# The 512-key tiles of P: transposed in the rounded type after a transfer from SBUF to SBUF

## The chip, the cores and the metric

The kernel runs on one core of a Trainium2 chip. The metric is the device time of one execution, in microseconds (us). Before the change it is 824.83 us, the median of 3 runs that lie between 823.99 and 824.9 us.

Five instruction streams run side by side: PE (TensorE, matmuls and their weight loads), DVE (VectorE), ACT (ScalarE), POOL (GpSimd) and SP (SyncE, which here only issues DMA transfers). Each works its own list strictly in the order in which it was written, and waits on semaphores for the others.

## The reference

Block-causal attention (blocks of 64 positions), then a feed-forward block whose gate comes from a convolution over three positions. All of it is float32, and the shapes are 8 batches, 8 heads, 576 positions, 64 features per head, and 1024 hidden features.

```python
scores = 1/sqrt(64) * q @ k.T                 # per batch and head: 576 x 576
scores = where(block_i >= block_j, scores, -1e9)
attn = softmax(scores) @ v                    # max taken off first, exp, divided by the row's sum
x = concat of the heads                       # 576 x 512 per batch
h = maximum(x @ w_in, 0)                      # 576 x 1024
conv = sum over k of conv_w[k] * h shifted by k - 1
out = (h * sigmoid(conv)) @ w_out             # 576 x 512
```

## The kernel before, in words

**Precision.** TensorE multiplies in the rounded type (float32r in the code, `F32R`), so most operands are held as a rounded part "h" and a remainder "l", and a product is the sum of two or three matmuls over these parts.

**Attention.** The work goes by pairs of heads. A head's queries are cut into blocks of 128: block i (0 to 3) sees 128(i+1) keys, so block 3 sees 512 keys; the last 64 queries of both heads of a pair form a fifth block of 576 keys. For a block, two matmuls make the scores in a PSUM bank (lines 709 and 711), DVE writes the mask (714) and takes the row maximum (717), ACT takes the exponential and its row sum (720) into an SBUF tile `p0` to `p4` in plain float32, DVE sums and inverts (671, 676), and POOL multiplies the tile by the inverse in place (682). These tiles are called P here. Then `one_bank` (from line 786) transposes P: TensorE takes each chunk of 128 keys as the stationary operand and an identity (`ident`, float32) as the moving one, with `is_transpose` set (791), into a PSUM bank; ACT evicts the bank as the rounded part (801) and DVE subtracts to get the remainder (804). The matmuls with the values read these (868). A tile of 512 keys is transposed in 4 chunks; there are 64 such tiles, one for each head and batch, in all 256 transposes out of some 800 at line 791.

**Stages.** The first batch is treated in two parts, queries 0 to 255 of all four pairs ("A") and then the rest ("B"), while the weights arrive and are decoded. The other 28 pairs are done whole. The 512-key tiles of the first batch belong to part B. The feed-forward matmuls of a batch (lines 936 and 993) are spread between the attention work of the next batch; those of the last batch end the program.

**What sets the order.** Each operation is entered in a plan with its engine, an estimated duration and latency, its dependences and a due time; `Plan.order` (line 94) then sorts all of it into one list per engine. The constants from line 224 on (`SLOT`, `OX`, `WOFF` and so on) set the due times. A tile taken from `one` has a single buffer, one from `two` has two, and the next user of a buffer depends on every user of the tile before it. Where the plan sees TensorE idle for longer than `LEAST` = 0.45 us, it puts in transposes of the identity that nobody reads (line 1110, called fillers here); there are 274 of them.

**DMA.** Nearly all transfers are issued from SP: the loads of q, k and v, the moves of rounded parts between partitions of SBUF (599, 608, 621) and the stores of the output (1006). A transfer that waits for its source holds up all that stand behind it on SP.

Of the kernel before, what the change touches and what calls it, by code (L numbers as in the profile page):

```python
# [193 lines left out]
def kernel(  # L194
# [26 lines left out]

    Q1 = 256

    SLOT, SLOTA, SLOTB = 10.87, 3.37, 5.12
    WOFF, WSTEP, WLEAD = 8.21, 4.0, 6.0
    WOFF2, WSTEP2 = 38.72, 3.23
    OXA, OPVA, OTA = 1.86, 3.32, 0.58
    OXB, OPVB, OTB = 5.65, 14.0, 3.99
    OX, OPV, OT = 8.41, 18.92, 6.21
    VLEAD, NLEAD, NB, CONV = 4.98, 4.48, 2.78, -20.45  # L230
    OFA, OFB, OF, OXS = 2.97, 9.83, 2.14, 1.25
    FA, FB = 51.86, 92.46
    TAIL1 = ('f', 's')
    TAIL2 = ('pt', 'tv')
    EBLK = (2,3)
    SKIP = 5.0
    LEAST, SPARE = 0.45, 0.2
    GROUPS = {"A": ((0, 1),), "B": ((2,), (3,)), None: ((0, 1, 2), (3,))}
    NORMS = {"A": (0,1), "B": (2,4), None: ()}
    VACT = True  # L240
    XDIRECT = True
    WDVE = ()
    WINDOW = 33.68

    cp = ctx.enter_context(tc.tile_pool(name="cp", bufs=1))
    p2 = ctx.enter_context(tc.tile_pool(name="p2", bufs=2))
# [43 lines left out]
    def c_pool(n, two_in=False):  # L290
        return 0.1 + n * 0.0022 if two_in else 0.16 + n / 1200.0

    ident = cp.tile([P, P], F32, tag="ident", name="ident")
    make_identity(nc, ident)
    nident = cp.tile([P, P], F32R, tag="nident", name="nident")
    nc.scalar.activation(out=nident, in_=ident, func=AF.Copy, scale=-1.0)
    wih = cp.tile([P, NCC, DFF], F32R, tag="wih", name="wih")
# [358 lines left out]
    def stage_s(ops, hh, at, part, shared):  # L656
# [9 lines left out]
        def finish(blocks, st, c0, t0):  # L666
            a, b_, w_ = c0 + blocks[0], c0 + blocks[-1] + 1, 2 if blocks[0] < 4 else 3

            def i1():
                x = 4 if blocks[0] == 4 else 4 + 2 * blocks[0]  # L670
                nc.vector.tensor_reduce(out=st.ap[:, a:b_],
                                        in_=st.ap[:, x:x + w_ * (b_ - a)].rearrange("p (n w) -> p n w", w=w_),
                                        op=ALU.add, axis=AX.X)

            def i2():
                nc.vector.reciprocal(st.ap[:, a:b_], st.ap[:, a:b_])  # L676

            o = pl.op(DVE, 0.15, i1, t0, deps=exps[4] if blocks[0] == 4 else [exps[x] for x in blocks], bufs=[st])
            o = pl.op(DVE, 0.12, i2, t0, deps=[o], bufs=[st])
            for x in blocks:  # L680
                def norm(pt=pb[x], col=c0 + x):
                    nc.gpsimd.tensor_scalar(out=pt.ap, in0=pt.ap, scalar1=st.ap[:, col:col + 1], scalar2=0.0,  # L682
                                            op0=ALU.mult, op1=ALU.add)

                w = 128 * (x + 1) if x < 4 else S
                if x in NORMS[part]:
                    def norm_a(pt=pb[x], col=c0 + x):
                        nc.scalar.activation(out=pt.ap, in_=pt.ap, func=AF.Copy, scale=st.ap[:, col:col + 1])  # L688

                    done[x] = pl.op(ACT, c_act(w, False, True), norm_a, t0 + 0.3, deps=[o], bufs=[st, pb[x]])  # L690
                    continue
                done[x] = pl.op(POOL, c_pool(w) + 0.08, norm, t0 + 0.3, deps=[o], bufs=[st, pb[x]])

        groups = GROUPS[part]
        for z, i in enumerate(i for g in groups for i in g):
            nk = 128 * (i + 1)
            pt = two([P, nk], F32, f"p{i}")
            pb[i] = pt
            t0 = at + (0.6 if part == "A" else 1.3) * z
            sb = bank("f" if part == "A" and i else "s")  # L700
# [74 lines left out]
    def stage_x(pbd, hh, at, part, shared):  # L775
# [10 lines left out]
        def one_bank(trs, rows, n, hi, lo, deps, t0, bufs_p, bufs_hi, bufs_lo, sub_ok, tag, shape):  # L786
            tb = bank(tag)

            def tr():
                for z, (x, c, kk, col) in enumerate(trs):  # L790
                    nc.tensor.matmul(tb.ap[0:kk, col:col + P], pb[x].ap[:, 128 * c:128 * c + kk], ident,  # L791
                                     start=(z == 0), stop=True, is_transpose=True, skip_group_check=True)

            o = pl.op(PE, len(trs) * 0.109, tr, t0, deps=deps, bufs=[tb] + bufs_p)

            def src():
                x = tb.ap[0:rows, 0:n]
# [348 lines left out]
```

## Time and profile before

| | |
|---|---|
| median of the runs | 824.83 us |
| the profiled execution's own time | 826.01 us |
| its span, first to last instruction | 824.2 us |
| PE busy / its weight loads busy | 805.8 us / 736.6 us |
| DVE / ACT / POOL busy | 658.5 / 634.0 / 437.9 us |
| granted TensorE clock, mean over the span | 0.995 |
| DMA: moved, mean rate | 96.09 MB, 117 GB/s |
| SP's DMA queue: share of the 16 engines | 47.3% |

A row of the profile names the line of the code, the engine, the operation, what is written and read (`w<-ident,p` is the transpose of P into a bank `w`), the shapes and the count, then busy time, the mean of one instruction in ns, and idle time ahead of it. Matmuls overlap each other, so the mean length of one (some 270 ns for a transpose) isn't what it costs; the distance from start to start is. That distance is read from the timeline, where equal neighbours are merged: n matmuls that together last T, each of length L, started (T - L)/(n - 1) apart.

### The profile page before, as it was taken

The page shows a single profiled execution, that of the slowest core. Times are in us where ns is not written, and L with a number is a line of the kernel's source. Part 1 is how long each engine was busy: PE and PEld are TensorE (multiplying, and loading weights), DVE is VectorE, ACT ScalarE, POOL GpSimd, SP SyncE. Part 2 cuts the span into 40 slices and gives each one's busy share as a digit, 9 for nine tenths or more (in the row PEclk, how much of TensorE's full clock was granted, in tenths as well). Part 3 has the DMA queues.
Part 4 walks back from the last instruction along what each step waited for, and adds up shares of the span by engine and source line. Part 5 has one row for each costly group of instructions (what it writes and reads, how often), then busy time and mean ns, then how long its engine had stood idle before and what let it go on. Part 6 is the DMA issues. An engine that isn't in the chain of part 4 may idle for free.

```text
span 824.2 us, 17518 instructions
## 1 busy us (share of the span) xinstructions
PE 805.8 (98%) x5531; PEld 736.6 (89%) x5531; DVE 658.5 (80%) x1945; ACT 634.0 (77%) x1800; POOL 437.9 (53%) x579
## 2 busy tenths in 40 slices
PE   7999899999999999999999999999999999999997
PEld 6888778988999989999999989999999989999996
DVE  5899887998997967889797967889797977887541
ACT  5789887887896967878796967878796967877651
POOL 2456566564565645546555645546565645645421
PEclk9999999999999999999999999999999999999999
DMA  9364756556555544444556444445556434430001
GB/s 234 113 155 104 183 159 157 131 126 147 146 119 145 117 103 107 106 113 114 145 119 146 108 113 103 106 114 117 145 119 144 116 91 113 93 99 14 14 26 40
DMA packets 168096, 96.09 MB, mean 117 GB/s; under 512 B 136748, under 2 KB 142404, under 8 KB 168004
## 3 DMA queue, kind: packets, MB, share of 16 engines
q1 hardware_dynamic: 165924, 94.44, 47.3%
q8 instruction: 45, 0.74, 0.4%
q10 hardware_dynamic: 2080, 0.52, 0.4%
q14 instruction: 47, 0.39, 0.2%
HBM read 38.82 MB, written 9.44 MB: 59 GB/s over the span
## 4 chain that ended last, share of the span: by engine, by line
PE 90%; DVE 3%; SPq 2%; ACT 2%; DMA 2%; issue 1%; POOL 0%; ACTq 0%; DVEq 0%
PE f L936 24%; PE f L993 21%; PE w L868 12%; PE w L791 10%; PE s L709 5%; PE s L711 5%; PE w L582 4%; PE w L993 3%; PE s L747 3%; PE s L936 2%; PE s L1110 1%; DMA xh<-in_moe_w_out_dram 1%; SPq L372 1%; DMA kn<-in_k_dram 1%; DMA ka<-kh 1%
## 5 line engine op out<-in xcount | busy, mean ns | idle before, releaser
L682 POOL TENSOR_SCALAR p<-p,st 128x512 f32<-128x512 f32 (+4 forms) x260 | 144.3, 570 | 158.6 <-DVE st L676 73.1
L974 POOL TENSOR_TENSOR gl<-t,gh 128x288 fp32r<-128x288 f32 (+2 forms) x128 | 103.9, 816 | 127.4 <-ACT gh L971 101.2
L720 ACT ACTIVATE p<-s,st 128x128 f32<-128x128 f32 (+1 forms) x248 | 131.2, 529 | 36.2 <-DVE st L717 31.0
L791 PE MATMUL w<-ident,p 128*128 128x128 f32 (+1 forms) x800 | 126.6, 275 | 1.9 <-DVE kl L589 1.4
L717 DVE TENSOR_REDUCE st<-s 128x1 f32<-128x128 f32 (+1 forms) x248 | 120.4, 486 | 4.0
L801 ACT ACTIVATE ptbh<-w 128x512 fp32r<-128x512 f32 (+2 forms) x192 | 94.5, 509 | 26.5 <-PE w L791 25.5
L791 PEld LDWEIGHTS w<-ident,p 128*128 128x128 f32 (+1 forms) x800 | 95.3, 140 | 12.9 <-ACT p L688 1.9
L993 PE MATMUL f<-woh,gh 128*128 128x512 f32 x248 | 105.8, 427 | 0.0
L936 PE MATMUL f<-xh,wih 128*128 128x290 f32 (+2 forms) x480 | 101.7, 312 | 0.4 <-ACT stage L1003 0.3
L804 DVE TENSOR_TENSOR ptbl<-w,ptbh 128x512 fp32r<-128x512 f32 (+1 forms) x144 | 89.9, 633 | 14.8 <-ACT ptbh L801 14.3
L936 PE MATMUL f<-xh,wil 128*128 128x290 f32 (+2 forms) x480 | 99.2, 310 | 0.0
L993 PE MATMUL f<-woh,gl 128*128 128x512 f32 x248 | 98.2, 396 | 0.0
L993 PE MATMUL f<-wol,gh 128*128 128x512 f32 x248 | 98.1, 395 | 0.0
L936 PE MATMUL f<-xl,wih 128*128 128x290 f32 (+2 forms) x480 | 96.0, 305 | 0.0
L711 PE MATMUL s<-kl,qz 128*128 128x128 f32 (+1 forms) x240 | 78.0, 325 | 0.0
L936 PEld LDWEIGHTS f<-xh,wih 128*128 128x128 f32 x480 | 74.1, 189 | 3.9 <-DVE t L967 0.6
L955 DVE SCALAR_TENSOR_TENSOR t<-f,cw,t 128x287 f32<-128x287 f32 (+3 forms) x120 | 59.0, 492 | 20.6 <-ACT t L951 19.4
L936 PEld LDWEIGHTS f<-xl,wih 128*128 128x128 f32 x480 | 73.8, 190 | 0.8
L936 PEld LDWEIGHTS f<-xh,wil 128*128 128x128 f32 x480 | 73.2, 190 | 0.3
L889 DVE TENSOR_TENSOR xt<-w,xt 64x256 f32<-64x256 f32 x112 | 51.3, 460 | 27.2 <-ACT xt L886 24.6
L886 ACT ACTIVATE xt<-w 64x256 f32<-64x256 f32 x112 | 44.8, 402 | 23.0 <-PE w L868 18.4
L868 PE MATMUL w<-ptbh,vv 128*128 128x320 f32 (+3 forms) x288 | 62.3, 320 | 0.0
(161 smaller groups left out, 2054.7 us busy)
## 6 DMA issues: line engine op xcount, KB each, us to landing
kn<-in_k_dram SPq DMA_DIRECT2D x64, 144.0 KB, 2.9
ka<-kh SPq DMA_DIRECT2D x64, 144.0 KB, 2.7
kb<-kh SPq DMA_DIRECT2D x64, 144.0 KB, 2.6
out_dram<-stage SPq DMA_DIRECT2D x36, 256.0 KB, 2.3
vn<-in_v_dram SPq DMA_DIRECT2D x64, 128.0 KB, 2.6
qn<-in_q_dram SPq DMA_DIRECT2D x56, 144.0 KB, 2.7
qa<-qh SPq DMA_DIRECT2D x28, 144.0 KB, 3.1
qa<-ql SPq DMA_DIRECT2D x28, 144.0 KB, 3.1
```

Of the source, the lines that this page charges most:

```text
L682: nc.gpsimd.tensor_scalar(out=pt.ap, in0=pt.ap, scalar1=st.ap[:, col:col + 1], scalar2=0.0, op0=ALU.mult, op1=ALU.add)
L711: nc.tensor.matmul(sb.ap[:, 0:nk], qz.ap[:, z:z + 128], kl.ap[:, 0:nk], start=False, stop=True)
L717: nc.vector.tensor_reduce(out=st.ap[:, i:i + 1], in_=sb.ap[:, 0:nk], op=ALU.max, axis=AX.X, negate=True)
L720: nc.scalar.activation(out=pt.ap[:, 0:nk], in_=sb.ap[:, 0:nk], func=AF.Exp, bias=st.ap[:, i:i + 1], accum_out=st.ap[:, 4 + 2 * i:5 + 2 * i])
L791: nc.tensor.matmul(tb.ap[0:kk, col:col + P], pb[x].ap[:, 128 * c:128 * c + kk], ident, start=(z == 0), stop=True, is_transpose=True, skip_ ...
L801: nc.scalar.activation(out=hi(), in_=src(), func=AF.Copy)
L804: nc.vector.tensor_tensor(out=lo(), in0=src(), in1=hi(), op=ALU.subtract)
L868: nc.tensor.matmul(tb.ap[0:m, q0 - qa:qb - qa], vv.ap[:, chunk(c), hh, w[ps_]], pm.ap[:, 128 * c + q0:128 * c + qb] if qa == 0 else pm.ap[ ...
L936: nc.tensor.matmul(fb.ap[:, 0:n2], wt[:, c, fs], xs[c][xi].ap[:, x0:x0 + n2], start=(n + c - c0 == 0), stop=(n + c - c0 == 3 * NCC - 1))
L955: nc.vector.scalar_tensor_tensor(out=t.ap[:, i0:no], in0=fb.ap[:, own + i0 - 1:own + no - 1], scalar=cw[:, f:f + 1], in1=t.ap[:, i0:no], o ...
L974: nc.gpsimd.tensor_tensor(out=gbuf[1].ap[:, f, carry:carry + no], in0=t.ap[:, 0:no], in1=gbuf[0].ap[:, f, carry:carry + no], op=ALU.subtract)
L993: nc.tensor.matmul(fb.ap[:, 0:DM], gbuf[a].ap[:, f, cs], w[:, f, :], start=(f == 0 and n == 0), stop=(f == NFC - 1 and n == 2))
```

## The change

P's tiles in `RAW`, which are those of 512 keys, get one step more. After POOL has normalized the tile, SP issues a transfer of all of it (128 partitions of 2 KB) from SBUF to SBUF, into a tile `pr3` that is declared in the rounded type; the bytes are the same. The transposes of that tile read `pr3` and a second identity, `rident`, in the rounded type, and write their PSUM bank through a view in that type. The tile `p3` now has one buffer in place of two, and `pr3` has one. What reads the bank afterwards is as it was.

The plan books 0.65 us on SP for the transfer and 2.6 us more until it has landed, and 0.087 us in place of 0.109 us for one of these transposes. The due times were set anew as well, and so the lists of all engines differ in many places.

```diff
-    SLOT, SLOTA, SLOTB = 10.87, 3.37, 5.12
+    SLOT, SLOTA, SLOTB = 10.69, 3.13, 5.12
...
+    RAW = (3,)
...
+    rident = cp.tile([P, P], F32R, tag="rident", name="rident")
+    nc.scalar.activation(out=rident, in_=ident, func=AF.Copy)
...
                 done[x] = pl.op(POOL, c_pool(w) + 0.08, norm, t0 + 0.3, deps=[o], bufs=[st, pb[x]])
+                if x in RAW:
+                    pr = one([P, w], F32R, f"pr{x}")
+
+                    def over(pt=pb[x], pr=pr):
+                        nc.sync.dma_start(out=pr.ap.bitcast(F32), in_=pt.ap)
+
+                    done[x] = pl.op(SP, 0.65, over, t0 + 1.0, deps=[done[x]], bufs=[pb[x], pr], lat=2.6)
+                    pb[x] = pr
...
-            pt = two([P, nk], F32, f"p{i}")
+            pt = (one if i in RAW else two)([P, nk], F32, f"p{i}")
...
-                    nc.tensor.matmul(tb.ap[0:kk, col:col + P], pb[x].ap[:, 128 * c:128 * c + kk], ident,
-                                     start=(z == 0), stop=True, is_transpose=True, skip_group_check=True)
-
-            o = pl.op(PE, len(trs) * 0.109, tr, t0, deps=deps, bufs=[tb] + bufs_p)
+                    to = tb.ap[0:kk, col:col + P]
+                    raw = x in RAW and pb[x].args[2] == F32R
+                    nc.tensor.matmul(to.bitcast(F32R) if raw else to, pb[x].ap[:, 128 * c:128 * c + kk],
+                                     rident if raw else ident, start=(z == 0), stop=True, is_transpose=True, skip_group_check=True)
+
+            o = pl.op(PE, len(trs) * (0.109 if trs[0][0] not in RAW else 0.087), tr, t0, deps=deps, bufs=[tb] + bufs_p)
```

The counts by kind are the same on both sides but for these: 256 transposes change their operands, SP has 64 transfers more, ACT has one copy more (`rident`), and the fillers go from 274 to 257. Three places show what moved. They lie around one tile, that of the first head in the third pair of the fifth batch; line numbers of the changed kernel are 4 to 14 higher.

PE, the rows up to the transposes of that tile, before (`s` banks take scores, `w_6986` and `w_6992` are banks for transposes, `p3_6898` is the tile):

```order
L709 MATMUL s_6963<-kb_6710,qb_6639 128x128
L711 MATMUL s_6963<-kl_6594,qz0_96 128x128
L993 MATMUL f_6969<-woh_85,gh_1138 128x512
L993 MATMUL f_6969<-wol_86,gh_1138 128x512
L993 MATMUL f_6969<-woh_85,gl_1189 128x512
L582 MATMUL w_6979<-ident_76,kn_6734 128x96 x3
L791 MATMUL w_6986<-ident_76,p0_6852 128x128
L791 MATMUL w_6986<-ident_76,p1_6866 128x128 x2
L791 MATMUL w_6992<-ident_76,p3_6898 128x128 x4
L709 MATMUL s_7003<-kb_6710,qb_6639 128x256
```

And in the changed kernel:

```order
L805 MATMUL w_7019<-ident_76,p0_6902 128x128
L805 MATMUL w_7019<-ident_76,p1_6916 128x128 x2
L721 MATMUL s_7029<-kb_6758,qb_6689 128x128
L723 MATMUL s_7029<-kl_6662,qz0_98 128x128
L1007 MATMUL f_7034<-woh_87,gh_1159 128x512
L1007 MATMUL f_7034<-wol_88,gh_1159 128x512
L1007 MATMUL f_7034<-woh_87,gl_1182 128x512
L586 MATMUL w_7045<-ident_76,kn_6814 128x96 x3
L721 MATMUL s_7053<-kb_6758,qb_6689 128x256
L723 MATMUL s_7053<-kl_6662,qz0_98 128x256
L805 MATMUL w_7060<-rident_81,pr3_6993 128x128 x4
```

The transposes of `p0` and `p1` moved ahead, and one pair of score matmuls of 256 keys now stands before the tile's transposes rather than behind them. Between the tile's own scores and these rows the two lists hold the same matmuls otherwise.

POOL at the same tile, before and then in the changed kernel (`gl` is the remainder of the gated activations, `st` the inverses):

```order
L974 TENSOR_TENSOR gl_1189<-t_6839,gh_1138 128x288
L682 TENSOR_SCALAR p0_6852<-p0_6852,st0_92 128x128
L682 TENSOR_SCALAR p1_6866<-p1_6866,st0_92 128x256
L682 TENSOR_SCALAR p2_6878<-p2_6878,st0_92 128x384
L682 TENSOR_SCALAR p3_6898<-p3_6898,st0_92 128x512
```

```order
L686 TENSOR_SCALAR p0_6902<-p0_6902,st0_94 128x128
L686 TENSOR_SCALAR p1_6916<-p1_6916,st0_94 128x256
L686 TENSOR_SCALAR p2_6930<-p2_6930,st0_94 128x384
L988 TENSOR_TENSOR gl_1182<-t_6893,gh_1159 128x288
L686 TENSOR_SCALAR p3_6954<-p3_6954,st0_94 128x512
```

A subtraction for the feed-forward block now stands between the normalization of `p2` and that of `p3`.

SP, from the loads of the values to the moves for the next pair of heads, before and in the changed kernel:

```order
L335 DMA vn_6792<-in_v_dram 64x2x64 x2
L319 DMA qn_6942<-in_q_dram 96x6x64 x2
L621 DMA qa_6961<-qh_6890 64x576
L621 DMA qa_6961<-ql_6900 64x576
L621 DMA qb_6983<-ql_6900 64x576
```

```order
L339 DMA vn_6838<-in_v_dram 64x2x64 x2
L701 DMA pr3_6883<-p3_6820 128x512
L701 DMA pr3_6993<-p3_6954 128x512
L625 DMA qa_7005<-qh_6977 64x576
L625 DMA qa_7005<-ql_6989 64x576
```

The transfers of two tiles, that of the head before and this one, stand between the loads of the values and the moves for the next pair, and the load of the following pair's q, which stood there, comes behind those moves.

More of the change, by code (lines that the diff above doesn't have):

```diff
@@ L222 @@
     Q1 = 256
-    SLOT, SLOTA, SLOTB = 10.87, 3.37, 5.12
[L225 to L232, printed above, removed]
+    SLOT, SLOTA, SLOTB = 10.69, 3.13, 5.12
+    WOFF, WSTEP, WLEAD = 6.38, 4.22, 5.72
+    WOFF2, WSTEP2 = 39.52, 3.2
+    OXA, OPVA, OTA = 3.87, 3.53, 0.33
+    OXB, OPVB, OTB = 4.55, 14.0, 3.99
+    OX, OPV, OT = 8.48, 18.92, 6.36
+    VLEAD, NLEAD, NB, CONV = 3.96, 7.21, 3.37, -20.45
+    OFA, OFB, OF, OXS = 2.97, 9.83, 2.14, 2.05
+    FA, FB = 61.7, 86.99
     TAIL1 = ('f', 's')
     TAIL2 = ('pt', 'tv')
+    RAW = (3,)
     EBLK = (2,3)
-    SKIP = 5.0
+    SKIP = 5.16
     LEAST, SPARE = 0.45, 0.2
@@ L242 @@
     WDVE = ()
-    WINDOW = 33.68
+    WINDOW = 36.23
     cp = ctx.enter_context(tc.tile_pool(name="cp", bufs=1))
```

## The prediction

> **What bounds the kernel now.** I read the page first, then the windows, to see in which stage TensorE is the bound.
>
> ```profile
> PE 805.8 (98%) x5531; PEld 736.6 (89%) x5531; DVE 658.5 (80%) x1945; ACT 634.0 (77%) x1800; POOL 437.9 (53%) x579
> PE   7999899999999999999999999999999999999997
> PE 90%; DVE 3%; SPq 2%; ACT 2%; DMA 2%; issue 1%; POOL 0%; ACTq 0%; DVEq 0%
> ```
>
> PE is busy in 98% of the span, and the chain of work that ended last runs over PE for 90%. "Busy" can hide waiting, so I split the span at 140 us, where the last long run of fillers has ended; the second answer is of the fillers (line 1110) alone, the third of PE's groups between 140 and 750 us.
>
> ```profile
> 0.00:140.00 140.00, 126.28 (x926) 111.26 (x927) 115.60 (x354) 110.60 (x301) 73.72 (x79) 0.98 0.64 157
> 140.00:750.00 610.00, 609.69 (x4213) 563.72 (x4212) 513.57 (x1528) 487.24 (x1413) 340.04 (x472) 1.00 0.50 118
> ```
>
> ```profile
> 0.00:140.00 140.00, 37.45 (x271) 32.62 (x271) 0.98 0.64 157
> 140.00:750.00 610.00, 0.52 (x3) 0.32 (x3) 1.00 0.50 118
> ```
>
> ```profile
> L791 PE MATMUL w<-ident,p 128*128 128x128 f32 (+1 forms) x683 | 106.4, 273 | 0.1
> ```
>
> The columns are the window, PE, its weight loads, DVE, ACT and POOL, each busy time and count, then clock and DMA. Up to 140 us PE idles for 14 us and runs 271 fillers: chains through the other engines set the pace there. From 140 to 750 us it is busy for 609.69 of 610 us with 3 fillers, its transposes waited 0.1 us in all, and the clock is full. What is left after 750 us is matmuls of the last batch. So a nanosecond taken off PE between 140 and 750 us comes off the end, as long as no new wait eats it; one taken off before 140 us mostly doesn't.
>
> **What one transpose costs now.** From the timeline, a group of four transposes with its weight loads and what follows:
>
> ```profile
> 404.32 0.49 PEld L791 LDWEIGHTS w<-ident,p 128*128 128x128 f32 x4
> 404.45 0.60 PE L791 MATMUL w<-ident,p 128*128 128x128 f32 x4
> 404.81 0.51 PE L936 MATMUL f<-xh,wil 128*128 128x290 f32 x2
> 409.69 0.41 PE L582 MATMUL w<-ident,qn 96*128 96x96 f32 x3
> ```
>
> ```profile
> L582 PE MATMUL w<-ident,qn 96*128 96x96 f32 x168 | 23.0, 245 | 0.4 <-issue 0.4
> ```
>
> One lasts 0.273 us, so four started (0.60 - 0.273)/3 = 0.109 us apart. The transposes of q (line 582, 0.245 us each) have as many weight columns, 128, but 96 moving ones: (0.41 - 0.245)/2 = 0.082 us. Per moving column that is 0.85 ns in both; so in float32 the moving side is the limit, and a float32 weight load of 128 columns needs no more than 0.082 us.
>
> **What one costs in the rounded type: the disputed term.** The trace of before has no such transpose. Three rows or pairs of rows bound it:
>
> ```profile
> 403.96 0.22 PE L709 MATMUL s<-ka,qa 128*128 128x128 f32 x1
> 404.02 0.27 PE L711 MATMUL s<-kl,qz 128*128 128x128 f32 x1
> 404.13 0.48 PE L936 MATMUL f<-xh,wil 128*128 128x290 f32 x2
> ...
> 70.79 0.53 PEld L808 LDWEIGHTS w<-ptbh,nident 128*128 128x128 f32 x4
> 70.91 0.56 PE L808 MATMUL w<-ptbh,nident 128*128 128x128 f32 x4
> ```
>
> ```profile
> L808 PEld LDWEIGHTS w<-ptbh,nident 128*128 128x128 f32 x56 | 7.8, 190 | 2.0 <-ACT ptbh L801 1.6
> ```
>
> The page writes f32 for both types here; lines 709, 711 and 808 multiply in the rounded one. A rounded matmul with 128 moving columns needs 0.06 us when its weights are in place (403.96 to 404.02). With weights of its own, the next starts 0.11 us on (to 404.13), and line 808's loads follow each other by (0.53 - 0.190)/3 = 0.113 us: the rounded weight load is the limit there, at 0.11 us. So 0.06 us is the floor, if in transpose mode the rounded load is as quick as the float32 one, and 0.111 us the ceiling, if it is as slow as at line 808. Both rows are equally near (the floor shares the mode of the load, the ceiling its type), and I take the middle, 0.086 us: 0.023 us saved, between 0.049 saved and 0.002 lost. A page of the Trainium skill, TensorE: Matmul & The Clock Gate, speaks against any gain in its section on LDWEIGHTS: a load takes the columns divided by 1.2 ns, 107 ns for 128. Line 808 agrees with it at 0.113 us and line 582 doesn't, with at most 0.082 us; held to strictly, it gives the second rival's time.
>
> **The change part by part.**
>
> Transposes. The tiles of 512 keys that POOL normalizes between 140 and 750 us, and the others of that line, stand in one row:
>
> ```profile
> L682 POOL TENSOR_SCALAR p<-p,st 128x512 f32<-128x512 f32 x54 | 37.8, 701 | 5.0 <-DVE st L676 4.9
> ```
>
> 54 tiles with 4 transposes are 216; 216 x 0.023 = **5.0 us** off the path (bounds: 10.6 off, 0.4 on). The other 40 run before 140 us and count nothing; their 0.9 us lie under the chains of that stage.
>
> Fillers. The lists have 17 fewer: 17 x 0.109 = **1.9 us** less idle time that is filled. This holds only if the idle time itself went, so I keep 0 to 3 us for it.
>
> The transfer's time. It moves 256 KB in 128 rows. Nearest rows, with the median from issue to landing:
>
> ```profile
> ka<-kh SPq DMA_DIRECT2D x64, 144.0 KB, 2.7
> out_dram<-stage SPq DMA_DIRECT2D x36, 256.0 KB, 2.3
> qa<-qh SPq DMA_DIRECT2D x28, 144.0 KB, 3.1
> ```
>
> ```profile
> 402.10 0.58 SPq L1006 DMA_DIRECT2D out_dram<-stage  x1
> 405.28 0.54 SPq L1006 DMA_DIRECT2D out_dram<-stage  x1
> 414.31 0.89 SPq L319 DMA_DIRECT2D qn<-in_q_dram  x2
> ```
>
> The same shape to DRAM takes 2.3 us, moves within SBUF 2.7 to 3.1. I take 2.7 us, 0.55 of which is the issue on SP. SP has room: between 405.82 and 414.31 us it issues nothing.
>
> Whether that is hidden. What hides it is the PE work between a tile's scores and its transposes. The chain of the tile shown in the part on the change, before:
>
> ```profile
> 431.91 0.39 PE L711 MATMUL s<-kl,qz 128*128 128x512 f32 x1
> 432.53 0.69 DVE L717 TENSOR_REDUCE st<-s 128x1 f32<-128x512 f32 x1
> 433.26 0.69 ACT L720 ACTIVATE p<-s,st 128x512 f32<-128x512 f32 x1
> 434.08 2.07 POOL L682 TENSOR_SCALAR p<-p,st 128x128 f32<-128x128 f32 x4 [0.16 <-PE w L868]
> 438.60 0.93 PE L791 MATMUL w<-ident,p 128*128 128x128 f32 x7
> 439.29 0.37 PE L709 MATMUL s<-kb,qb 128*128 128x256 f32 x1
> 439.61 0.39 PE L993 MATMUL f<-woh,gh 128*128 128x512 f32 x1
> ```
>
> The four normalizations end at 436.15, 4.24 us after the scores start; the tile's transposes are the last four of the seven, at 438.60 + 3 x 0.109 = 438.93, 7.0 us after. So 2.8 us were spare, and nothing waited. In the changed list one pair of 256-key scores is added ahead (439.29 to 439.61, 0.32 us): 7.3 us. But POOL now has a subtraction ahead of the tile's normalization, whose price has this row:
>
> ```profile
> L974 POOL TENSOR_TENSOR gl<-t,gh 128x288 fp32r<-128x288 f32 x92 | 74.4, 812 | 91.1 <-ACT gh L971 71.5 <-issue 19.1
> ```
>
> 4.24 + 0.81 + 2.7 = 7.75 us, against 7.3: PE would wait about 0.4 us. This is the tightest place; its pattern comes twice (fifth and seventh batch), which puts **0.8 us** back. Counted in the same way on the lists, with each matmul at its distance from the timeline, the other heads of the stage have 7.7 to 10.8 us between scores and transposes, mostly about 9. A usual chain, that of another head:
>
> ```profile
> 407.98 0.39 PE L711 MATMUL s<-kl,qz 128*128 128x512 f32 x1
> ...
> 411.76 0.70 POOL L682 TENSOR_SCALAR p<-p,st 128x512 f32<-128x512 f32 x1
> ```
>
> It has its norm at 412.46, 4.5 us after the scores, and with the transfer needs 7.2 us: 1.8 us spare. If that cover were gone, each of the 54 tiles would show its 2.7 us on PE.
>
> What stands behind the transfer on SP are the moves of q for the next pair, and the scores at line 709 wait for these:
>
> ```profile
> 437.09 0.51 SPq L621 DMA_DIRECT2D qa<-qh  x1
> ```
>
> ```profile
> 448.98 0.22 PE L709 MATMUL s<-ka,qa 128*128 128x128 f32 x1
> ```
>
> In the old run they went out at 437.09, after the norm's end at 436.15 us, and were needed 11.9 us later, so a transfer ahead of them costs nothing. SP's 64 issues of some 0.55 us, 35 us, lie in such gaps as the one above. The copy for `rident` falls into the start, where the loads are waited for: nothing, and on the path less than the 0.69 us of the 512-column row of ACT.
>
> Sum against the profiled execution (826.01 us, 1.2 us above the median): -5.0 - 1.9 + 0.8 = -6.1 us, 819.9 us. Against the median of 824.83 us: **818.7 us**.
>
> **The rivals.**
>
> 1. *The rounded load is quick in transpose mode*: 0.06 us each. 216 x 0.049 = 10.6 us; 824.8 - 10.6 - 1.9 + 0.8 = 813.1 us. For it: line 582's loads, in that mode, keep within 0.082 us. Against: no rounded load anywhere in the trace is below 0.11.
> 2. *No gain on PE*: the load stays at 0.111 us as at line 808, or the rounded type is moved at float32's rate, 0.109. 824.8 + 0.4 - 1.9 + 0.8 = 824.1 us.
> 3. *The transfer is the new wait, slower*: PE works its list in order, so a tile that lands late stops all of PE at the 54 places. The price is 54 times the mean shortage; with 6.1 us to lose, it turns the sign at 0.11 us of mean shortage. It would come where SP is just issuing a pair of loads ahead of the transfer (0.89 us for two at 414.31), the transfer lands in 3.1 us and a subtraction of 0.81 us has slipped in on POOL: 0.9 + 0.4 + 0.8 = 2.1 us, 0.3 more than the usual spare. A mean shortage of 0.3 us gives 824.8 - 6.9 + 16.2 = 834.1 us. Against: SP's idle stretch, and the distance from scores to transposes, whose median on the lists goes from 6.8 to 9.0 us.
>
> 4. *The single buffer of `p3` stops the early stage.* There the scores of two heads come close:
>
> ```profile
> 58.94 0.40 PE L711 MATMUL s<-kl,qz 128*128 128x512 f32 x1
> ...
> 63.45 0.40 PE L711 MATMUL s<-kl,qz 128*128 128x512 f32 x1
> ```
>
> 4.5 us apart, and an exponential starts 1.35 us after its scores (431.91 to 433.26), so the second one would find `p3` taken until 7.2 us after the first scores: it waits 7.2 - 4.5 - 1.35 = 1.35 us, and ACT with it, on 8 heads up to 11 us: 824.8 - 6.9 + 11 = 828.9 us. Against: the fillers of that stage show idle time that can take it. Its chance is in that of rival 3.
>
> **How the numbers follow.** The forecast has 45% (its own range 815 to 822 us), the quick load 20%, no gain 20%, the two late cases 15%. The range from 811 to 826.5 us takes in the first three and little of the last. A measurement of this kernel can tell 0.2%, 1.65 us, from no change, so faster means below 823.2 us: nearly all of the first two and, since 824.1 us lies so near the border, 7 points of the third, 72%. Within 0.2%: 12%. Slower: 16%.
>
> **What would show it.** Starts of the new transposes: 0.086 us apart if the forecast is right, 0.06 or 0.11 if a rival is. PE between 140 us and the last batch: still no wait on `pr3`, but for two tiles with some 0.4 us; rows "PE w <- DMA pr3" with over 6 us in all would mean rival 3. The transfer: 2.3 to 3.1 us to landing. The first 140 us: a 512-key score in the first whole pair not later than now. The forecast falls if the starts are at 0.11 or if the steady stage shows waits for the transfer.

## The result

The changed kernel takes 834.85 us (median of 4 runs, 832.25 to 837.3) beside 824.87 us of the kernel before on the same chip (823.99 to 825.07): 1.0123 times the time, 95% interval 1.0087 to 1.0158. It is slower by 10 us, 1.2%. The prediction was 818.7 us, and its range ended at 826.5 us. The profiled execution took 836.21 us; its span is 834.4 us, 10.2 us more than before.

The page of the changed kernel: busy time, then PE in 40 slices, then the chain that ended last by engine.

```profile
PE 806.5 (97%) x5514; PEld 726.5 (87%) x5514; DVE 654.7 (78%) x1945; ACT 636.8 (76%) x1801; POOL 435.4 (52%) x579
...
PE   8998889999999999999999999999999999999998
...
PE 76%; ACT 8%; DMA 6%; SPq 5%; DVE 2%; issue 2%; POOL 1%; ACTq 0%; POOLq 0%; DVEq 0%
```

PE is still busy for 97%, and the slices still read 9, so neither shows the loss. The chain does: PE's share in it fell from 90% to 76%, while DMA and SP's queue together went from 4% to 11% and ACT from 2% to 8%. Next the windows, split at the same 140 us, and then the fillers alone (now line 1124) in the same windows:

```profile
0.00:140.00 140.00, 124.52 (x888) 105.42 (x888) 114.69 (x354) 109.63 (x300) 71.13 (x77) 0.96 0.68 168
140.00:750.00 610.00, 601.62 (x4155) 549.40 (x4155) 500.54 (x1499) 481.01 (x1385) 333.96 (x465) 1.00 0.57 142
```

```profile
0.00:140.00 140.00, 35.81 (x242) 30.15 (x242) 0.96 0.68 168
140.00:750.00 610.00, 2.19 (x15) 1.66 (x15) 1.00 0.57 142
```

In the stage where PE sets the end it now idles for 610 - 601.62 = 8.4 us, where it idled for 0.3 us, and it runs 15 fillers in place of 3. What it waits for stands in PE's waits, and the spread of the transfer in the rows of its tile:

```profile
PE w L805 <- DMA pr<-p: 6.4, 8, 1.9
```

```profile
L701 SPq DMA_DIRECT2D pr<-p x64: 465/518/559, 53.9 to 761.8; - x64
...
DMA to landing us min/median/max: 2.3/2.4/5.0
```

The transposes waited for the transfer 8 times, 6.4 us in all and up to 1.9 us at once. The prediction had two waits of 0.4 us, and gave "over 6 us in all" as the mark of its third rival. The median of 2.4 us from issue to landing is even better than the 2.7 us that the prediction took, but the longest is 5.0 us. Two tiles from the timeline, SP's rows and then PE's, show both cases. The first came in time:

```profile
606.28 0.51 SPq L701 DMA_DIRECT2D pr<-p  x1
...
610.32 0.46 PE L805 MATMUL w<-rident,pr 128*128 128x128 f32 x4
610.62 0.35 PE L721 MATMUL s<-kb,qb 128*128 128x256 f32 x1
...
640.39 1.01 SPq L323 DMA_DIRECT2D qn<-in_q_dram  x2
641.50 1.07 SPq L323 DMA_DIRECT2D kn<-in_k_dram  x2
642.68 0.53 SPq L701 DMA_DIRECT2D pr<-p  x1
...
645.13 0.34 PE L723 MATMUL s<-kl,qz 128*128 128x384 f32 x1
647.37 0.51 PE L805 MATMUL w<-rident,pr 128*128 128x128 f32 x4 [1.90 <-DMA pr<-p]
```

The second one's normalization ended at 641.01 us. SP was issuing the loads of q and k just then, and came to the transfer 1.67 us later; the transfer landed 4.56 us after its issue began, and all of PE stood for 1.9 us. Both were needed for a wait of that size: issued without the 1.67 us, the tile would have been some 0.2 us late, and landing in 2.4 us it would have been in time.

To see what makes a transfer late, I put all of them into classes by what their packets met: loads of q or k issued just ahead, and packets of the queues that the page calls "instruction" (the engines' own code being fetched):

```profile
q8 instruction: 44, 0.72, 0.4%
...
q14 instruction: 49, 0.40, 0.2%
```

| what the transfer met | median landing us (54 with a recorded landing) | longest | tiles of all 64 | PE's waits ahead of them us |
|---|---|---|---|---|
| neither | 2.36 (31) | 4.87 | 29 | 0.2 |
| loads of q or k | 3.24 (11) | 4.56 | 13 | 2.8 |
| a code fetch | 3.58 (8) | 4.72 | 12 | 2.5 |
| both | 4.36 (4) | 4.95 | 10 | 5.5 |

The last column is worked out from start-to-start distances on PE, each compared with the distance that its kind of matmul has where nothing is waited for; it adds to 11.0 us, some 10 of them after 150 us. ("By distances" below means this.) It is more than the 6.4 us of the waits' row, because that row names one releaser only. The landings are classed by what their whole flight met, the tiles by what the time up to the transposes met, hence 31 and 29. The 4.87 us among those that met neither is of 81.5 us, in the early stage, where two transfers of weights and three moves within SBUF, issued ahead of it, landed after its issue.

### The profile page after: what moved, and what is told of

It is laid out like the page before. It is cut to its first block, busy times and chain, and to the rows that moved or that the text cites. A ratio compares the mean times of both kernels' runs of the same rounds, so it can differ in the third digit from the quotient of the medians.

```text
span 834.4 us, 17685 instructions
## 1 busy us (share of the span) xinstructions
PE 806.5 (97%) x5514; PEld 726.5 (87%) x5514; DVE 654.7 (78%) x1945; ACT 636.8 (76%) x1801; POOL 435.4 (52%) x579
## 4 chain that ended last, share of the span: by engine, by line
PE 76%; ACT 8%; DMA 6%; SPq 5%; DVE 2%; issue 2%; POOL 1%; ACTq 0%; POOLq 0%; DVEq 0%
PE f L950 19%; PE f L1007 19%; PE w L882 10%; PE w L805 8%; DMA pr<-p 5%; PE s L721 4%; PE s L723 4%; PE w L1007 3%; PE w L586 3%; PE s L759 3%; PE s L950 2%; SPq L625 1%; ACT p L732 1%; ACT p L773 1%; SPq L323 1%
## 5 line engine op out<-in xcount | busy, mean ns | idle before, releaser
L729 DVE TENSOR_REDUCE st<-s 128x1 f32<-128x128 f32 (+1 forms) x248 | 118.6, 484 | 3.0
L950 PE MATMUL f<-xh,wih 128*128 128x290 f32 (+2 forms) x480 | 99.6, 311 | 0.7 <-DVE t L981 0.5
L805 PE MATMUL w<-ident,p 128*128 128x128 f32 (+1 forms) x544 | 91.2, 275 | 2.9 <-ACT ptbl L826 1.2
L950 PE MATMUL f<-xh,wil 128*128 128x290 f32 (+2 forms) x480 | 92.3, 305 | 0.0
L950 PE MATMUL f<-xl,wih 128*128 128x290 f32 (+2 forms) x480 | 91.6, 302 | 0.0
L805 PEld LDWEIGHTS w<-ident,p 128*128 128x128 f32 (+1 forms) x544 | 64.4, 139 | 15.2 <-ACT p L692 3.3
L950 PEld LDWEIGHTS f<-xl,wih 128*128 128x128 f32 x480 | 72.0, 189 | 0.5
L978 ACT ACTIVATE t<-t 128x288 f32<-128x288 f32 (+2 forms) x128 | 56.4, 442 | 7.9 <-DVE t L973 6.8
```

The source lines that it names most:

```text
L729: nc.vector.tensor_reduce(out=st.ap[:, i:i + 1], in_=sb.ap[:, 0:nk], op=ALU.max, axis=AX.X, negate=True)
L805: nc.tensor.matmul(to.bitcast(F32R) if raw else to, pb[x].ap[:, 128 * c:128 * c + kk], rident if raw else ident, start=(z == 0), stop=True ...
L950: nc.tensor.matmul(fb.ap[:, 0:n2], wt[:, c, fs], xs[c][xi].ap[:, x0:x0 + n2], start=(n + c - c0 == 0), stop=(n + c - c0 == 3 * NCC - 1))
```

## The experiments

**First theory: the transfers land late and PE waits; order and transposes do what was predicted.** Its rival: the new order of the lists is itself the loss. Four kernels, each planned anew by the same planner.

`order_only` takes the new due times and no tile takes the new way:

```diff
-    RAW = (3,)
+    RAW = ()
```

> The new due times alone: no tile is in RAW, so no transfer, float32 transposes, two buffers of p3. Late landing: the transposes cost what they did, the lists have 49 fillers fewer than before (225 for 274), so within 1% below to 0.3% above the time before: 817 to 827 us. Rival, bad order: most of the 10 us loss stays, 830 us or more.

Measured: 834.06 us (832.04 to 835.05) beside 824.48; ratio 1.0108 [1.009, 1.0127].

`no_transfer` has POOL write its normalized tile, rounded, straight into `pr3`:

```diff
...
-                        nc.sync.dma_start(out=pr.ap.bitcast(F32), in_=pt.ap)
...
+                        nc.gpsimd.tensor_scalar(out=pr.ap, in0=pt.ap, scalar1=st.ap[:, col:col + 1], scalar2=0.0,
+                                                op0=ALU.mult, op1=ALU.add)
...
```

> The changed kernel without the transfer: POOL's normalization writes the 512-key tile straight into the rounded-type tile, so P of these tiles is rounded there and its remainder is zero; the rapid transposes stay, all due times are those of the changed kernel. Late landing (my theory): the transposes are worth 256 x (0.109 - 0.084) = 6.4 us and nothing waits for a transfer, so 816 to 821 us, and no wait of some 10 us ahead of the rident transposes. Rival, the new order itself is bad (the due times): it stays above 828 us, since order and due times are kept. Rival, more DMA traffic slows the other transfers: that traffic is gone too, so it also gives 816 to 821 us; the run with the idle transfer tells these two apart.

Measured: 828.97 us (825.47 to 830.45) beside 824.48; 1.0044 [1.0024, 1.0064].

`idle_transfer` issues the transfers but transposes the tile as before, in float32 (and the plan books 0.109 us for each of these transposes again):

```diff
-                    done[x] = pl.op(SP, 0.65, over, t0 + 1.0, deps=[done[x]], bufs=[pb[x], pr], lat=2.6)
-                    pb[x] = pr
+                    pl.op(SP, 0.65, over, t0 + 1.0, deps=[done[x]], bufs=[pb[x], pr], lat=2.6)
...
```

> All 64 transfers are issued as in the changed kernel but nobody reads pr3: the transposes read p3 in float32 as before and don't wait for the landing (p3 keeps one buffer). Late landing: PE waits for no transfer; dearer transposes (+6.4 us) against waits of 11 us that go: 826 to 831 us, that is below the changed kernel and at most 3 us above the run with the new due times alone. Rival, traffic and SP's issues slow the rest: it stays 6 us or more above the run with the new due times alone, 833 us or more.

Measured: 836.16 us (833.65 to 838.53); 1.0147 [1.012, 1.0173].

`change_old_due_times` is the change with the constants `SLOT`, `SLOTA` and the others as they were before it.

> The transfer and the rapid transposes with the due times of before. Late landing: the distance from scores to transposes isn't made for a transfer, so the waits ahead of the rident transposes are as long as in the changed kernel or longer; the lists have 320 fillers (46 more than before, 5.0 us): 833 to 845 us. Rival, bad order: with the old due times the 6.4 us of the transposes show, 816 to 822 us.

Measured: 840.44 us (838.6 to 842.62); 1.019 [1.0169, 1.0211].

The first theory fell as it stood: without any transfer the new due times alone were 9.6 us slower, and `no_transfer`, which should have been faster than before, was 4.5 us slower. `idle_transfer` lies in its rival's range as well, and only `change_old_due_times` in the theory's. But none of them shows what the order of the *change* costs, since the planner makes another order each time: `order_only` has 225 fillers, `no_transfer` 247, `idle_transfer` 263, `change_old_due_times` 320, the change 257. These four kernels without the change's own lists spread over 829 to 840 us. For the same reason the 2.1 us by which `idle_transfer` lies above `order_only`, with overlapping runs, are no price of traffic and issues: its lists hold 38 fillers more. `change_old_due_times` is the slowest of the four, so with the transfer, setting the due times anew was worth 5.6 us to this planner.

**Second round: keep the lists word for word, change one thing at a time.** `same_order_f32` has exactly the changed kernel's lists, without the transfers, and float32 transposes that read `p3` in place:

```diff
-                        nc.sync.dma_start(out=pr.ap.bitcast(F32), in_=pt.ap)
+                        pass
...
-                    nc.tensor.matmul(to.bitcast(F32R) if raw else to, pb[x].ap[:, 128 * c:128 * c + kk],
-                                     rident if raw else ident, start=(z == 0), stop=True, is_transpose=True, skip_group_check=True)
+                    nc.tensor.matmul(to, (pb[x].real or pb[x]).ap[:, 128 * c:128 * c + kk],
+                                     ident, start=(z == 0), stop=True, is_transpose=True, skip_group_check=True)
```

> The order of the changed kernel without the transfers and with the float32 transposes of before (two real buffers of p3): what the order alone is worth against the time before. From the sums of the stages (non-work time early and late in the run with the new due times alone, 7 to 8 us over before): 828 to 833 us, and 6.4 us above the run without the wait if 84 against 109 ns is the whole worth of the rapid transposes. If the order were neutral: 824 to 826 us.

Measured: 828.88 us (827.84 to 829.28); 1.0047 [1.0028, 1.0065].

`same_order_no_wait` has those lists and no transfers too, but keeps the rounded transposes, with `p3` declared in the rounded type from the exponential on.

> Instruction for instruction the order of the changed kernel, but for the 64 transfers, which are left out: the 512-key tile is of the rounded type from the exponential on (so P of these tiles is rounded there and its remainder is zero), and its transposes read it in place, rapidly as in the changed kernel. The difference from the changed kernel is thus the transfer alone, waits and traffic. Late landing: the 10 us of waits ahead of the rident transposes after 150 us go, 822 to 826 us. Rival, the new order alone makes the loss: 831 us or more.

Measured: 825.01 us (822.28 to 827.11, 10 runs) beside 824.67 (14 runs); 1.0000 [0.9984, 1.0016].

`old_order_rapid` is the kernel before, its lists untouched, with the 512-key tiles in the rounded type from the exponential on and their transposes against `rident`:

```diff
...
-            pt = two([P, nk], F32, f"p{i}")
+            pt = two([P, nk], F32R if i == 3 else F32, f"p{i}")
...
```

> The kernel before, order and buffers untouched, but the 512-key tiles are of the rounded type from the exponential on (rounded there, remainder zero), and are transposed with rident; no transfer. If the 25 ns per transpose come off the path in the stage that PE bounds: 216 x 0.025 = 5.4 us less, 818 to 820.5 us. Rival, other waits take up what PE gains (DVE or ACT near their bound): 822 to 825 us.

Measured: 821.27 us (820.57 to 822.18); 0.9957 [0.9942, 0.9972].

The times of the first two lie in the ranges that were forecast for them; `old_order_rapid` lies between its theory and its rival, 0.8 us above the first. That the rounded transposes would bring 6.4 us between the first two failed: they brought 3.9 us. Together the three split the change:

| lists of | float32 transposes | rounded, no transfer | rounded, with the transfer |
|---|---|---|---|
| the kernel before | 824.7 | 821.3 | not run |
| the changed kernel | 828.9 | 825.0 | 834.85 |

The order costs 4.2 us, the rounded transposes bring 3.9 us (3.4 in the old order), and the transfer costs 9.8 us: 4.2 - 3.9 + 9.8 = 10.1. That they add up to the result follows from the way they are formed; what each is worth hangs on its own two medians, whose runs spread over 1.4 to 5 us.

With the transfer went its issue, its traffic, its wait and the single buffers. Since `same_order_no_wait` and the changed kernel have the same PE list, matmul for matmul, each distance from start to start can be set against its counterpart. In the two profiled executions the changed kernel's are 10.7 us longer in all after 150 us: 9.9 us of it stand directly ahead of the groups of rounded transposes, 0.9 us within the groups, and the rest of PE together is 0.2 us shorter. Before 150 us, where the single buffers were feared, they are 1.3 us shorter. So the loss is the wait for the transfer, and not what its traffic or the single buffers do to other work; the next round tells what makes it late.

The windows from 140 to 750 us of `same_order_f32`, `same_order_no_wait` and `old_order_rapid`, one fence each, show the same:

```profile
140.00:750.00 610.00, 609.09 (x4207) 561.19 (x4206) 507.38 (x1517) 486.26 (x1405) 337.61 (x469) 1.00 0.51 119
```

```profile
140.00:750.00 610.00, 608.78 (x4229) 559.52 (x4228) 510.64 (x1528) 488.92 (x1415) 339.93 (x471) 1.00 0.51 120
```

```profile
140.00:750.00 610.00, 609.84 (x4239) 563.53 (x4239) 516.46 (x1537) 489.00 (x1423) 343.73 (x478) 1.00 0.50 118
```

Without the transfer PE is idle for 0.9 and 1.2 us in this stage in the new order, and for 0.2 us in the old. The counts tell what the order costs. The change's lists have 242 fillers up to 140 us and 15 after it. Up to 750 us the kernel before had run 926 + 4213 - 274 = 4865 matmuls that are not fillers; `same_order_f32`, with 889 up to 140 us, had run 889 + 4207 - 257 = 4839. It is 26 behind, at 610/4213 = 0.145 us each 3.8 us. Of these 26, 8 were missing at 140 us already. The other 18 are 2.6 us: the 12 fillers that were added in the bound stage take 1.3 us, and PE's longer idle time (0.9 for 0.3 us) 0.6 us. Why the early stage is behind, and where the last 0.7 us are, I could not settle.

**Third round: why the transfers land late.** Either SP comes to them late, or the 16 DMA engines are shared with something. `transfer_on_act` issues them from ACT's queue:

```diff
-                        nc.sync.dma_start(out=pr.ap.bitcast(F32), in_=pt.ap)
+                        nc.scalar.dma_start(out=pr.ap.bitcast(F32), in_=pt.ap)
```

> The changed kernel with the same order, but the transfer is issued from ACT's queue at the place that the plan gave it in time, so it stands in no SP list and in a ring of its own. If the waits come from SP's list and from the loads of q and k ahead in the same ring: the wait from norm's end to issue (median 0.5, up to 2.0 us) and the landings of 3.2 us behind loads shrink, and the time falls to 826 to 831 us. If they come from the shared DMA engines and the code fetches (landings of 3.6 to 4.9 us): landings stay as they are and the time is 832 to 838 us. ACT's list grows by 64 issues, and a norm that is late holds up ACT, which could make it slower still.

Measured: 841.7 us (839.4 to 849.74); 1.0231 [1.017, 1.0292]. PE's waits for the transfer, and its landing:

```profile
PE w L805 <- DMA pr<-p: 7.1, 9, 1.6
```

```profile
DMA to landing us min/median/max: 2.2/2.8/5.4
```

The time from the normalization's end to the issue fell from a median of 0.5 us to 0.03 us, and nothing was won: the landings keep their classes (2.31 us alone, 3.50 with loads, 3.30 with a code fetch, 4.55 with both), and PE's waits by distances are 10.0 us. So the place in SP's list is not the main cause. The time is 7 us longer than the changed kernel's, above both ranges. The profiled execution's span is 4.5 us longer: distance by distance, what stands ahead of the rounded transposes is 0.8 us less, and PE's other work lost 4.2 us after 150 us and 1.7 us before. ACT now works 64 issues as well; whether that is the reason was not tested. The Trainium skill states in "Trainium Kernel Development and Optimization", Key Constraints, that transfers issued from SP, ACT and POOL run on the same 16 engines and interleave, and that another queue saves only the time of issuing. These landings agree: 3.50 us behind loads from ACT's queue, 3.24 us from SP's.

`small_loads` keeps the changed kernel as it is, and lets the loads of q and k from the second whole pair on fetch a sixth of their bytes:

```diff
-                    nc.sync.dma_start(out=n.ap[0:w, 0:r_, j, :],
-                                      in_=src[b, h0 + j, tok, :].rearrange("(r p) d -> p r d", r=r_))
+                    c = slice(0, 1) if p > NP else slice(0, r_)
+                    nc.sync.dma_start(out=n.ap[0:w, c, j, :],
+                                      in_=src[b, h0 + j, tok, :].rearrange("(r p) d -> p r d", r=r_)[:, c, :])
```

> The changed kernel in its own order, but from the second whole pair on the loads of q and k bring only the first of their six rows per partition (a sixth of the bytes and packets; the rest of the tile keeps old values, so the attention of later batches is computed from wrong q and k, at the same cost). If the loads ahead of the transfer on the engines are half of its late landings: the landings behind loads fall from 3.2 to about 2.4 us, only those that meet a code fetch stay late; of 11.0 us of waits ahead of the rident transposes (2.8 with loads alone, 5.5 with both, 2.5 with fetches alone) some 4 to 5 are left: 826 to 831 us. If the loads don't matter: 832 to 838 us and landings behind loads stay above 3 us.

Measured: 826.38 us (median of 10 runs; nine within 825.1 to 828.78, one at 834.5) beside 824.74; 1.0032 [1.001, 1.0053]. Its group row, then the landing:

```profile
L806 PE MATMUL w<-rident,pr 128*128 128x128 f32 x256 | 31.0, 244 | 1.4 <-DMA pr<-p 0.7 <-DVE st L676 0.3
```

```profile
DMA to landing us min/median/max: 2.3/2.4/4.5
```

Nothing moved in the lists, every transfer is still there, and 8.5 of the 9.8 us are gone. A transfer behind loads now lands in 2.36 us like any other, and PE's waits by distances fell from 11.0 to 2.5 us, more than half of these at code fetches. Smaller loads could have sped up other work as well, but they did not: distance by distance against the changed kernel, 7.8 us went ahead of the rounded transposes after 150 us, 0.5 us within their groups, and the rest of PE changed by 0.1 us. SP still came to a transfer up to 2.2 us late, since it issues as many loads as before: a late issue alone is mostly hidden, and it is the loads' traffic that costs. This is the run that shows the mechanism: the transfer shares the DMA engines with the loads issued ahead of it, and PE stands for the difference.

`loads_behind` leaves the computation whole: where a load of q or k stood on SP within four issues and 3 us ahead of a transfer, it now stands behind it.

```diff
...
+            for x in reversed(sp[max(0, z - 4):z]):
+                if "load_nat" in x.fn.__qualname__ and o.start - x.start < 3.0:
+                    held.append(x)
...
```

> The changed kernel, complete, with one thing moved: where a pair of loads of q or k stands right ahead of a transfer on SP (within 3 us in the plan), the transfer now goes first and the loads follow it. All other lists are the same, row for row. If those loads are what makes the landings late (the run with small loads lost 8.5 us of waits): landings without a code fetch are back at 2.4 us, the waits ahead of the rident transposes fall from 11 to 3 to 5 us, 827 to 830 us. Rival: the loads, now held back by a transfer that waits for POOL, come too late for their own transposes, and PE waits at line 586 instead: 831 us or more.

Measured: 831.92 us (829.47 to 835.3) beside 825.55; 1.0093 [1.0066, 1.012]. The landing of its profiled execution, and PE's waits:

```profile
DMA to landing us min/median/max: 2.3/2.4/4.3
```

```profile
PE w L818 <- DMA pr<-p: 1.9, 4, 0.7
```

In the profile the waits are nearly gone (3.8 us by distances), and its span is 827.7 us, 6.7 below the change's. But the profiled execution was the quickest of four, and the median is only 2.9 us below the change, with overlapping runs; it lies in the rival's range. What the rival named is not in the profile: PE waits 0.7 us in all at the transposes of q and k, and never for a load. The order on SP matters in the way the theory says; how much of the 9.8 us it can win back stays open.

`longer_latency_planned` tells the planner 3.6 us in place of 2.6 us, so that it leaves more room itself:

```diff
-                    done[x] = pl.op(SP, 0.65, over, t0 + 1.0, deps=[done[x]], bufs=[pb[x], pr], lat=2.6)
+                    done[x] = pl.op(SP, 0.65, over, t0 + 1.0, deps=[done[x]], bufs=[pb[x], pr], lat=3.6)
```

> The changed kernel, but the plan books 3.6 in place of 2.6 us until the transfer has landed, with the same due times. The waits ahead of the rident transposes fall from 11 us to 4 or less, since only landings over 4.1 us miss then; but the plan finds no work for the time (its lists have 324 fillers, 67 more than the changed kernel's, 7.3 us): 830 to 837 us. If a longer distance alone mends it: 822 to 828 us.

Measured: 841.75 us (838.43 to 845.85); 1.0206 [1.0164, 1.0249], slower than both theories had it. PE's waits for the transfer did go (3.4 us by distances, against 11.0), but the price came elsewhere. The windows:

```profile
0.00:140.00 140.00, 124.42 (x867) 108.28 (x868) 111.26 (x332) 103.89 (x282) 66.44 (x70) 0.91 0.65 161
140.00:750.00 610.00, 605.36 (x4184) 554.19 (x4184) 500.92 (x1500) 478.67 (x1384) 337.38 (x466) 1.00 0.58 143
```

PE's idle time in the steady stage fell from 8.4 to 4.6 us, but of the 324 fillers 47 now stand in this stage, in place of 15, and take 3.5 us more: its matmuls that are not fillers are 4184 - 47 = 4137, where the changed kernel's were 4155 - 15 = 4140. So waits became fillers and nothing was won there. The loss is in the early stage: by 140 us, with the other 277 fillers, PE had run 867 - 277 = 590 matmuls that are not fillers, where the changed kernel had run 888 - 242 = 646, and 56 at 0.145 us are 8.1 us, the whole difference of the two spans (842.4 to 834.4 us). DVE, ACT and POOL are behind there as well, with 332, 282 and 70 operations for 354, 300 and 77. Room that is planned for every tile delays the early stage, where the chains through the other engines set the pace. The granted clock of that window is also lower in this execution, 0.91 for 0.96; what part of the delay that makes was not told apart.

**Last: what the rounded transposes are worth by themselves.** `old_order_all_rapid` is the kernel before with every tile of P in the rounded type from the exponential on, all transposes of P against `rident`, and no transfer.

> The kernel before in its own order, with all P tiles (not the 512-key ones alone) of the rounded type from the exponential on and transposed with rident; no transfer; P is rounded everywhere and its remainder is zero. 256 rapid transposes brought 3.4 us of 6.4 by count, those in the first 140 us bring nothing; 544 more at the same share: 7 to 11 us less than with the 512-key tiles alone, 810 to 815 us. If other engines bound it by now: 816 to 821 us.

Measured: 815.64 us (814.92 to 816.52); 0.9889 [0.9872, 0.9905], the fastest of all. It pays with precision: P is rounded ahead of its transposition, so the remainder that the kernel before carries along is zero. The group row:

```profile
L794 PE MATMUL w<-rident,p 128*128 128x128 f32 x768 | 93.1, 241 | 1.6 <-DVE ptbl L807 0.2 <-POOL p L684 0.2
```

The time lies between the theory's range and the rival's. 768 transposes at 25 ns less would be 19 us; 9.1 us came out. The rival, other engines, is not the reason: the list is that of the kernel before, matmul for matmul, and set against each other the distances within the groups of transposes are 19.6 us shorter in all, those from a group's last transpose to the matmul behind it 11.2 us longer and the next ones 2.9 us shorter, while all the rest changed by 0.7 us. In float32 the matmul behind a group starts 28 ns after the last transpose, in the rounded type 85 ns after it (medians). So a good part of what a group wins it gives back at its end.

## Why the prediction was wrong, step by step

**What bounds the kernel** held: PE's idle time from 140 to 750 us rose by 8.1 us and its fillers there by 1.7 us, and the span by 10.2 us.

**"What one costs in the rounded type"** was right. The new transposes start 84 ns apart (median of the 192 distances within groups), and 86 ns had been taken as the middle of 60 and 111; the float32 ones still start 109 ns apart. A load follows the one before it by 86 ns. The page of the Trainium skill that the prediction weighed, TensorE: Matmul & The Clock Gate, section LDWEIGHTS, would have 107 ns. In transpose mode the trace does not agree. With the starts at 84 ns the second rival fell.

**"Transposes", 5.0 us taken off the path**: the mechanism held, and the runs with equal lists measured a fifth to a third less, 3.9 us and 3.4 us. The sum took four times 23 ns a tile, as if each transpose kept the next matmul off by its own distance. The prediction's rows show that the last of a group doesn't: from 404.45 to 404.81 us four float32 transposes took 0.36 us and not 4 x 0.109. In the rounded type the end of a group costs more, as told above: a group of four takes 355 ns from its first start to that of the matmul behind it in the kernel before and 302 ns in `old_order_rapid` (medians), 53 ns less, and one step later some 15 ns more are won. For 54 tiles that is 2.9 to 3.7 us. That the early 40 transposes bring nothing was right: in `old_order_rapid` PE's distances before 150 us add up to the same as before.

**"Fillers", 1.9 us off**: wrong in sign. The order as a whole costs 4.2 us. The step took the count of fillers, 17 fewer, for time won. But 29 went from before 140 us, where they cost nothing, and 12 were added after it, where each costs its 0.109 us, 1.3 us of the 4.2. The order itself had no other term in the sum. A count of fillers says nothing until it is split by the stage in which they stand. The prediction's own first rows had made that split for the kernel before.

**"The transfer's time", 2.7 us, and "Whether that is hidden", 0.8 us back**: here the prediction failed, and 9.8 us stand in place of 0.8. Every landing that it used was a median, and the transfer's median was even better. The cover it reckoned, 1.8 us, was there: 39 of the 55 tiles after 150 us waited no more than 0.1 us by distances. PE works its list in order, so a tile that is late costs its whole shortage and one that is early wins nothing: what counts is the upper end. That end could be read before. The rows of the tile `ka` in the kernel before, moves within SBUF from the same queue:

```profile
L621 SPq DMA_DIRECT2D ka<-kh x64: 467/590/1833, 46.7 to 722.9; - x64
...
DMA to landing us min/median/max: 2.3/2.7/4.4
```

Against 1.8 us of usual spare with 2.7 us, a landing of 4.4 us leaves 0.1 us, and a wait on SP of 1.7 us ahead of it leaves a shortage of 1.6 us. Classed as above, those moves took 2.62 us alone and 3.51 us with a code fetch. The place that the prediction called tightest, the first head in the third pair of the fifth batch, did wait, 0.2 us, but not as reckoned: its normalization ended 3.8 us after its scores, where 5.05 had been added up, and the transfer met a code fetch and took 3.6 us. Its twin in the seventh batch did not wait; the 1.9 us fell on the head right behind that one, which no step had singled out.

**"SP has room"** held on the average and failed in the places that count: in the steady stage SP came to a transfer up to 2.0 us after its source was ready, in the cases read here behind the loads of q and k. By `transfer_on_act` that alone was not the loss.

**Rival 3** came true, at 834.1 us within a microsecond, yet for part of its reasons; that the number fits so well is luck. It had the loads ahead on SP, a landing of 3.1 us and a subtraction on POOL. The runs show the loads, but more by their traffic than by their issue, landings up to 5 us, and code fetches, which no step had. And its 16.2 us of waits were too many, while the order's 4.2 us were missing from it and the fillers' 1.9 us were counted as won. With 15% for it and the fourth rival, the chance was too low: the spread of the landings was in the trace of before.

**Rival 4**, the single buffer, was not seen. Before 150 us PE's waits and fillers rose by 1.6 us, and in `same_order_no_wait`, where `p3` has two buffers again, by 2.9 us. The first 512-key score of the whole pairs, at 131.97 us before, came at 132.59 us in the changed kernel, 0.6 us later than the prediction allowed, but with two buffers it came later still, at 133.89 us.

Taken together: the forecast of 818.7 us, 1.1 us for the transposes, 1.9 + 4.2 us for the fillers and the order, and 9.0 us for the transfer make 834.9 us.

## What to carry to other kernels

Where an engine works in order and is the bound, price a new transfer on its path by its longest landing and not by its median, and look at what is issued ahead of it on any queue: here landings behind loads were as late from ACT's queue as from SP's. Price a group of instructions up to the start of what follows it, and not by the distance within it alone. Split every count of idle or filler instructions by stage before turning it into time. And when a planner makes the lists, test a part of a change with the lists held fixed: what the runs planned anew (829 to 840 us) owed to their edit and what to their lists could not be told apart.

## What the runs showed of the hardware

- Code being fetched seems to delay data. The two queues of the page moved 0.72 + 0.40 = 1.1 MB in packets of 16 and 8 KB. A 16-KB packet held its DMA engine for 0.9 to 1.9 us (median 1.15), where a 2-KB packet of the transfer takes some 0.09 us; a transfer raises its semaphore 16 times, and has landed with the last of them. At 418.42 us a transfer went out with nothing issued ahead of it for 5.5 us (loads of q followed 1.8 us behind it), a 16-KB fetch took 1716 ns on one engine, and the landing took 4.72 us. That the one caused the other is inferred from the packets' times and the classes above; no run took the fetches away.
- Rounded weight loads of 128 columns follow each other by 86 ns in transpose mode (median, line 805), and by 110 ns outside it (line 822).
- The matmul behind a group of float32 transposes starts 28 ns after the last of them, and its own successor 217 ns later where 136 is usual (line 936 of the kernel before); behind rounded transposes these are 88 and 204.5 ns (`old_order_rapid`).
- A transfer from SBUF to SBUF of 128 rows of 2 KB lands in 2.36 us (median) when it meets neither loads of q and k nor a code fetch, and in 2.31 us when ACT issues it.
